# Two cached attentions at one decode step: from 217 tile loads to one stream in 62 KiB rows

## The chip, the cores and the metric

The kernel runs on one core of a Trainium2 chip. The metric is the device time of one execution in microseconds; three timed runs of the kernel before gave 1029.24, 1029.28 and 1032.6 us (median 1029.28 us). The engines are named as the profile names them: PE is TensorE (PEld its weight loads), DVE is VectorE, ACT is ScalarE, POOL is GpSimd, SP is SyncE, which here only issues DMAs. All data is float32.

## The reference, cut to what matters

Two attention blocks read one query token `x` (448 values). Block A has 16 heads with 16 key and value caches; block B has 16 query heads over 8 caches, so that two heads share one. A sigmoid gate mixes both outputs.

```
g = sigmoid((x * gate_w).sum())
for each block:                       # A: 16 caches, B: 8 caches, two heads each
    q = x @ wq                        # 448 -> 16 heads of 256
    scores = q . k_cache * 256**-0.5  # 8192 keys a head
    p = softmax(scores)
    o = p @ v_cache                   # 8192 values a head
    out = concat(o) @ wo              # 4096 -> 448
return g * out_A + (1 - g) * out_B
```

Each cache of one head is 8192 x 256 floats, 8 MiB, and there are 24 key caches and 24 value caches. With the weights that makes 432 MB, each byte of which is read once and used in one or two multiplications.

## The kernel before, in words

The work goes in 8 steps (`NS`). A step `s` holds one cache of B with its two heads (called unit 2) and two heads of A (units 0 and 1), in this order: 2, 0, 1. A cache is cut into 4 tiles (`NT`) of 2048 keys or values: 128 partitions of 4096 floats, 16 KiB a partition and 2 MiB a tile. So the loop `for i in range(N + 1)` (L343) has 96 rounds; in each, SP issues the load of key tile i and of value tile i-1, and now and then the projection weights `wq` (with 14 KiB a partition for a step) and the output weights `wo`. All these loads go into one ring of 11 slots of 16 KiB a partition (`slot`, L74). SP takes the loads in the order in which the program names them and waits ahead of each until its slot is free and an earlier load has landed; at most eight are under way.

A key tile is scored on PE (`scores`, L170). The keys lie turned in memory, so that a matmul with the 32-wide query weights `qb` gives 512 scores to each of four row groups. After each tile DVE takes the minimum (L183) and caps it (L185), ACT exponentiates (L187), and DVE turns the result (L190) into weights for the value matmuls (`attend`, L194, L203). Every tile has a minimum of its own; `combine` and `column` (L232, L265) weight the tiles' sums against each other once a unit has all four. `take` copies the sums out of PSUM, `project_o` makes a column of 256 out of them, and `emit` (L291) multiplies this with `wo` into `Y`. Blocks A and B go the same way.

At the end of the program the last value tile of A is loaded in three pieces (`LAST_CUT`) and the last `wo` in seven: three quarters of it as one load, the last quarter in loads of 96, 12, 8, 6, 4 and 2 partitions (`LAST_ROWS`, L368), 3584 bytes a partition each.

Of the kernel before, what the change touches and what calls it, by code (L numbers as in the profile page):

```python
# [14 lines left out]
P = 128  # L15
# [3 lines left out]
NCOL = SK // P  # L19
# [7 lines left out]
NT = NCOL // ROWS  # L27
BLK = 32
NB = ROWS
R = 4  # L30
OFF = -1.0e5
SLOTS = 11
WQ = (2 * KF + 1) * DH
UNITS = [2, 0, 1]
LAST_CUT = [8, 4, 4]
HEAD_AT = {2: 0, 0: 2, 1: 3}
LAST_ROWS = [96, 12, 8, 6, 4, 2]
# [3 lines left out]
def kernel(  # L41
    ctx: ExitStack,
    tc: tile.TileContext,
    x: bass.AP,
    gate_w: bass.AP,
    a_k: bass.AP,
    a_v: bass.AP,
    b_k: bass.AP,
    b_v: bass.AP,
    wq: bass.AP,  # L50
    wo: bass.AP,
# [8 lines left out]
    ps_sc = ctx.enter_context(tc.tile_pool(name="ps_sc", bufs=2, space=PSUM))  # L60
    ps_o = ctx.enter_context(tc.tile_pool(name="ps_o", bufs=3, space=PSUM))
# [4 lines left out]

    def heads(u):
        return 2 if u[1] == 2 else 1

    def of(u, a, b):  # L70
        s, r = u
        return b[s] if r == 2 else a[2 * s + r]

    def slot(shape, name):  # L74
        t = ring.tile([P, ROWS * DH], F32, name="slot")
        n = 1
        for d in shape:
# [21 lines left out]
    row_of = const.tile([P, R], F32, name="row_of")
    nc.vector.tensor_reduce(row_of, pos.rearrange("p g r -> p r g"), axis=AX.X, op=OP.add)  # L100
    MASK, CAP = {}, {}
    for M in (2, 1):
        MASK[M] = const.tile([P, R // M], F32, name=f"mask{M}")
        nc.vector.tensor_reduce(MASK[M], row_of.rearrange("p (t m) -> p t m", m=M), axis=AX.X, op=OP.add)

        CAP[M] = const.tile([P, R // M], F32, name=f"cap{M}")
        nc.vector.tensor_scalar(CAP[M], MASK[M], 3.0e38, OFF, op0=OP.mult, op1=OP.add)
# [30 lines left out]
    Y = ps_y.tile([P, YN], F32, name="Y")

    def prepare():  # L140
        clear(Y, YN)
        gp = ps_s.tile([1, 1], F32, name="sm")
        for c in range(KF + 1):
            nc.tensor.matmul(gp, xs[:, c:c + 1], gw[:, c:c + 1], start=(c == 0), stop=(c == KF))
        ge = const.tile([1, 1], F32, name="ge")
        nc.scalar.activation(ge, gp, AF.Exp, scale=-1.0)
        nc.vector.tensor_scalar(ge, ge, 1.0, None, op0=OP.add)
        nc.vector.reciprocal(gate[:, 0:1], ge)
        nc.vector.tensor_scalar(gate[:, 1:2], gate[:, 0:1], -1.0, 1.0, op0=OP.mult, op1=OP.add)

    KT, VT, ST, PR, O, GS, SEL, OB, OC = ({} for _ in range(9))

    def project(u, w):

        s, r = u
        M = heads(u)
        q = ps_s.tile([P, 2, 2], F32, name="sm")
        n = 2 * DH
        for m in range(M):
            h = m if r == 2 else r  # L160
            for e in range(2):
                for c in range(KF):
                    at = c * n + h * DH + e * P
                    nc.tensor.matmul(q[:, e, m:m + 1], w[:, at:at + P], xs[:, c:c + 1], start=(c == 0), stop=False)  # L164
                at = KF * n + e * P
                nc.tensor.matmul(q[:, e, m:m + 1], w[:, at:at + P], xs[:, KF + h:KF + h + 1], start=False, stop=True)  # L166
        qb = QB[s % 2, r]
        nc.vector.tensor_scalar(qb[:, :, 16:16 + M], q[:, :, :M], -scale, None, op0=OP.mult)  # L168

    def scores(u, t, kt):  # L170
        M = heads(u)
        if t == 0:
            ST[u] = small.tile([P, 2, NT], F32, name="st", bufs=3)
        sc = ps_sc.tile([P, NB * BLK], F32, name="sc")
        qb = QB[u[0] % 2, u[1]]
        for e in range(2):
            for g in range(NG):
                at = 16 - R * g - t * M % R
                nc.tensor.matmul(sc[32 * g:32 * (g + 1), :], qb[:, e, at:at + 32], kt[:, e, g, :],  # L179
                                 start=(e == 0), stop=(e == 1), skip_group_check=True)  # L180
        st = ST[u]
        mn = small.tile([P, 1], F32, name="mn")
        nc.vector.tensor_reduce(mn, sc, axis=AX.X, op=OP.min)  # L183
        tt = t % (R // M)
        nc.vector.tensor_tensor(st[:, 0, t:t + 1], mn, CAP[M][:, tt:tt + 1], op=OP.min)  # L185
        px = small.tile([P, NB * BLK], F32, name="px")
        nc.scalar.activation(px, sc, AF.Exp, bias=st[:, 0, t:t + 1], scale=-1.0, accum_out=st[:, 1, t:t + 1])  # L187
        pr = small.tile([P, NB * BLK], F32, name="pr")

        nc.vector.transpose(pr.rearrange("p (q r k) -> p q k r", r=BLK, k=2),  # L190
                            px.rearrange("p (q k c) -> p q k c", c=BLK, k=2))
        PR[u, t] = pr.rearrange("p (q c) -> p q c", c=2 * BLK)

    def attend(u, t, j0, n, vt):  # L194
        M = heads(u)
        part, tt = divmod(t, R // M)
        if tt == 0 and j0 == 0:
            O[u, part] = ps_o.tile([P, 2 * DH], F32, name="o")
            clear(O[u, part], 2 * DH)
        pr = PR[u, t]  # L200
        for j in range(j0, j0 + n, 2):
            g = j // 2 % NG
            nc.tensor.matmul(O[u, part][32 * g:32 * (g + 1), :], pr[:, j // 2, :2 * NG * R], vt[:, j - j0:j - j0 + 2, :],  # L203
                             start=False, stop=(tt == R // M - 1 and j >= NB - 2 * NG), skip_group_check=True)

    def take(u, t, last=False):

        M = heads(u)
        part, tt = divmod(t, R // M)
        if tt != R // M - 1:  # L210
            return
        o = O.pop((u, part))
        ob1 = small.tile([P, DH], F32, name="ob1")
        ob = small.tile([P, DH], F32, name="ob", bufs=4)
        if last:
            nc.scalar.activation(ob1, o[:, DH:], AF.Copy)  # L216
            nc.vector.tensor_copy(ob, o[:, :DH])  # L217
            OB[u] = [(ob, SELH[0]), (ob1, SELH[1])]
        else:
            nc.scalar.activation(ob1, o[:, DH:], AF.Copy, scale=half[:, 1:2])  # L220
            nc.vector.scalar_tensor_tensor(ob, o[:, :DH], half[:, 0:1], ob1, op0=OP.mult, op1=OP.add)  # L221
            OB.setdefault(u, []).append((ob, None))
# [254 lines left out]
```

## Time and profile before

| | before |
|---|---|
| median of three runs | 1029.28 us |
| profiled execution, first to last instruction | 1027.5 us |
| what lies around it (median less span) | 1.8 us |
| bytes read from HBM | 432.0 MB |
| rate over the span; in its middle | 420 GB/s; 427 GB/s |
| PE, DVE, ACT busy | 65%, 21%, 10% |
| mean granted TensorE clock | 0.767 |

For the profiled execution the record holds its span and no separate time. How to read it: a DMA of 128 rows is spread over 16 DMA engines, and a "packet" is what one engine moves as one piece: a row of a load, or a 4-byte semaphore update. "Share of 16 engines" is the time that packets took against 16 times the stretch; packets of one engine can overlap a little, so that a share may be over 100%. "GB/s" is what was moved. In groups of instructions, a fp32 matmul is two PE instructions, so `x16` is 8 matmuls of the program.

### The profile page before, as it was taken

The numbers are of one execution on the slowest core, as the hardware profiler recorded it, in microseconds if no ns is written. First come the engines' busy times: TensorE is split into PE (matmuls) and PEld (weight loads), VectorE is DVE, ScalarE is ACT, GpSimd is POOL, SyncE is SP. The second block draws the span as 40 slices with busy tenths as digits, with TensorE's granted clock in tenths as the row PEclk, the third lists the DMA queues.
The fourth block names the chain that finished last, engine by engine and source line by source line (L and its number), as shares of the span: only waits on it lengthen the run. The fifth ranks groups of instructions, "written<-read, shape, count | busy, mean of one in ns | idle before, by whom it ended". The sixth has DMA issues, their size and how long they took to land.

```text
span 1027.5 us, 10697 instructions
## 1 busy us (share of the span) xinstructions
PE 665.1 (65%) x4493; PEld 247.8 (24%) x4493; DVE 215.3 (21%) x650; ACT 98.7 (10%) x258; POOL 0.6 (0%) x6
## 2 busy tenths in 40 slices
PE   5669665696556855567556685556856568555656
PEld 3316111251112411133111251113311123111112
DVE  2121212222212212122121121221212112122222
ACT  1010001000010001000010010100101001010000
POOL 0000000000000000000000000000000000000000
PEclk9777776767766887678786688878787878887877
DMA  9999999999999999999999999999999999999996
GB/s 381 428 427 427 427 425 429 427 426 428 424 429 425 427 425 428 428 428 425 425 428 425 427 427 426 426 428 427 427 429 426 426 426 427 425 427 428 425 428 251
DMA packets 30903, 432.71 MB, mean 421 GB/s; under 512 B 3720, under 2 KB 3720, under 8 KB 4360
## 3 DMA queue, kind: packets, MB, share of 16 engines
q1 hardware_dynamic: 30568, 432.03, 99.3%
q8 instruction: 36, 0.59, 0.2%
q14 instruction: 11, 0.09, 0.0%
q10 hardware_dynamic: 288, 0.00, 0.0%
HBM read 432.02 MB, written 0.00 MB: 420 GB/s over the span
## 4 chain that ended last, share of the span: by engine, by line
DMA 97%; PE 2%; issue 0%; DVE 0%; SPq 0%; ACT 0%
DMA slot<-in_a_v_dram 57%; DMA slot<-in_a_k_dram 15%; DMA slot<-in_b_v_dram 13%; DMA slot<-in_b_k_dram 11%; PE o L203 1%; PE sc L179 0%; PE sm L164 0%; PE sm L286 0%; PE Y L296 0%; PE sm L166 0%; SPq L320 0%; DVE ob L217 0%; SPq L308 0%; ACT ob L216 0%; PE sm L270 0%
## 5 line engine op out<-in xcount | busy, mean ns | idle before, releaser
L203 PE MATMUL o<-slot,pr 128*32 128x512 f32 x1536 | 264.1, 816 | 205.0 <-DMA slot<-in_a_v_dram 139.7
L179 PE MATMUL sc<-slot,qb 128*32 128x512 f32 x1536 | 260.1, 807 | 145.9 <-DMA slot<-in_b_k_dram 84.4
L203 PEld LDWEIGHTS o<-slot,pr 128*32 128x32 f32 x1536 | 57.2, 132 | 377.5 <-issue 193.2
L183 DVE TENSOR_REDUCE mn<-sc 128x1 f32<-128x512 f32 x96 | 66.4, 691 | 376.2 <-PE sc L179 376.1
L187 ACT ACTIVATE px<-sc,st 128x512 f32<-128x512 f32 x96 | 66.0, 688 | 773.7 <-DVE st L185 773.7
L179 PEld LDWEIGHTS sc<-slot,qb 128*32 128x32 f32 x1536 | 54.6, 129 | 253.9 <-issue 239.3
L190 DVE STREAM_TRANSPOSE pr<-px 128x512 f32<-128x512 f32 x96 | 68.4, 713 | 89.0 <-ACT px L187 89.0
L164 PEld LDWEIGHTS sm<-xs,slot 128*128 128x128 f32 x384 | 61.7, 239 | 32.1 <-issue 25.3
L164 PE MATMUL sm<-xs,slot 128*128 128x1 f32 x384 | 65.5, 286 | 5.7 <-DMA slot<-in_wq_dram 5.7
L221 DVE SCALAR_TENSOR_TENSOR ob<-o,half,ob 128x256 f32<-128x256 f32 x31 | 14.9, 480 | 97.2 <-ACT ob L220 97.2
L166 PE MATMUL sm<-xs,slot 128*128 128x1 f32 x128 | 27.6, 285 | 0.0
L286 PEld LDWEIGHTS sm<-sel,ob 128*128 128x128 f32 x124 | 21.3, 248 | 20.5 <-issue 20.5
L278 DVE COPY sel<-sm 128x1 f32<-128x1 f32 (+1 forms) x23 | 3.7, 160 | 102.1 <-PE sm L270 102.1
L166 PEld LDWEIGHTS sm<-xs,slot 128*128 128x128 f32 x128 | 24.8, 240 | 0.0
L220 ACT ACTIVATE ob<-o,half 128x256 f32<-128x256 f32 x31 | 14.7, 474 | 103.9 <-PE o L203 72.6
L270 PEld LDWEIGHTS sm<-one,wr 1*128 1x128 f32 x96 | 16.4, 241 | 30.9 <-issue 29.2
L286 PE MATMUL sm<-sel,ob 128*128 128x2 f32 (+1 forms) x124 | 22.9, 298 | 0.0
L168 DVE TENSOR_SCALAR qb<-sm 128x2 f32<-128x2 f32 (+1 forms) x24 | 3.9, 162 | 79.7 <-PE sm L166 79.7
L270 PE MATMUL sm<-one,wr 1*128 1x1 f32 x96 | 18.5, 292 | 1.8 <-DVE wr L258 1.8
L187 ACT ACTIVATION_READ_ACCUMULATOR px<-sc,st 128x1 f32 x96 | 18.5, 193 | 0.0
L185 DVE TENSOR_TENSOR st<-mn,cap 128x1 f32<-128x1 f32 x96 | 15.3, 160 | 3.3
L136 PE MATMUL o<-zero 128*128 128x512 bf16 x32 | 15.7, 490 | 0.0
(48 smaller groups left out, 104.6 us busy)
## 6 DMA issues: line engine op xcount, KB each, us to landing
slot<-in_a_k_dram SPq DMA_DIRECT2D x64, 2048.0 KB, 38.9
slot<-in_a_v_dram SPq DMA_DIRECT2D x63, 2048.0 KB, 39.2
slot<-in_b_k_dram SPq DMA_DIRECT2D x32, 2048.0 KB, 39.1
slot<-in_b_v_dram SPq DMA_DIRECT2D x32, 2048.0 KB, 38.6
slot<-in_wq_dram SPq DMA_DIRECT2D x7, 1792.0 KB, 38.0
slot<-in_wo_dram SPq DMA_DIRECT2D x7, 1792.0 KB, 39.2
slot<-in_wq_dram SPq DMA_DIRECT2D x2, 896.0 KB
slot<-in_wo_dram SPq DMA_DIRECT2D x1, 1344.0 KB, 29.4
```

What stands on the lines that cost most here:

```text
L136: nc.tensor.matmul(t[:, :n], zero[:, :P], zero[:, :n], start=True, stop=False, skip_group_check=True)
L164: nc.tensor.matmul(q[:, e, m:m + 1], w[:, at:at + P], xs[:, c:c + 1], start=(c == 0), stop=False)
L166: nc.tensor.matmul(q[:, e, m:m + 1], w[:, at:at + P], xs[:, KF + h:KF + h + 1], start=False, stop=True)
L179: nc.tensor.matmul(sc[32 * g:32 * (g + 1), :], qb[:, e, at:at + 32], kt[:, e, g, :], start=(e == 0), stop=(e == 1), skip_group_check=True)
L183: nc.vector.tensor_reduce(mn, sc, axis=AX.X, op=OP.min)
L185: nc.vector.tensor_tensor(st[:, 0, t:t + 1], mn, CAP[M][:, tt:tt + 1], op=OP.min)
L187: nc.scalar.activation(px, sc, AF.Exp, bias=st[:, 0, t:t + 1], scale=-1.0, accum_out=st[:, 1, t:t + 1])
L190: nc.vector.transpose(pr.rearrange("p (q r k) -> p q k r", r=BLK, k=2), px.rearrange("p (q k c) -> p q k c", c=BLK, k=2))
L203: nc.tensor.matmul(O[u, part][32 * g:32 * (g + 1), :], pr[:, j // 2, :2 * NG * R], vt[:, j - j0:j - j0 + 2, :], start=False, stop=(tt == R ...
L221: nc.vector.scalar_tensor_tensor(ob, o[:, :DH], half[:, 0:1], ob1, op0=OP.mult, op1=OP.add)
L270: nc.tensor.matmul(cl[:, a, m:m + 1], WR[M][:, m, a].rearrange("p c x k -> p (c x k)"), one, start=True, stop=True)
L286: nc.tensor.matmul(oc[:, e, :M], ob[:, e::2], sel, start=(k == 0), stop=(k == len(terms) - 1))
```

## The change

The program is written anew around one input. The host lays every cache tile and weight block in the order of use into one flat array, `stream`; each load takes the next 15872 floats a partition (63488 bytes, `FILL`), whatever lies in them. There are 52 such loads, and then two slots that are filled in four pieces each (`TAIL`): 22528, 16384, 16384 and 7680 bytes a partition, and 5376, 3584, 1344 and 448. Every piece has 128 rows. The ring has 3 slots of 62 KiB a partition. The load into a slot is issued when the last item in the slot's earlier content has been used. `pieces` finds for an item (a tile, a weight block) the one, two or more parts of slots in which it lies.

The order of the items is written out in `order()`: in the steps after the first, A's key tiles come one in three or four items, between value tiles of A and tiles of B, and in the first step one in two or three.

Scores of A are made by DVE: the keys lie as rows, `tensor_tensor` multiplies a tile in place with the query (spread over all partitions by PE, in PSUM), and `tensor_reduce` sums 256 products to a score. All four tiles of a head stand in one 128x64 tile `s`. B's scores stay on PE, but all four tiles write one PSUM bank (rows 2t and 2t+1 of each group). So minimum, exponential and turning come once a head pair and no longer once a tile, with one minimum for all keys of a head; `combine`, `column` and the masks are gone, and the sum is divided out by `rz` in `narrow`. The queries are now made with `x` as the weights and `wq` as the moving operand, 512 columns a matmul. The last `wo` is used block by block as its pieces land.

The diff, cut to its core:

```diff
-SLOTS = 11
-UNITS = [2, 0, 1]
-LAST_CUT = [8, 4, 4]
-LAST_ROWS = [96, 12, 8, 6, 4, 2]
+FILL = 31 * UNIT
+SLOTS = 3
+TAIL = [[11 * UNIT, 8 * UNIT, 8 * UNIT, 2 * UNIT + 896], [1344, 896, 336, 112]]
...
+def order():
+    out = [("wq", 0, 0, 0)]
...
+        if s == 0:
+            out += k(0, 0) + k(2, 0, 1) + k(0, 1) + k(2, 2) + k(0, 2) + k(2, 3) + k(0, 3)
+            out += v(2, 0, 1) + k(1, 0) + v(2, 2, 3) + k(1, 1) + v(0, 0, 1) + k(1, 2) + v(0, 2)
+            out += k(1, 3) + v(0, 3) + [("wq", 1, 0, 0)]
+            continue
+        out += k(0, 0) + v(1, 0, 1, of=s - 1) + k(0, 1) + v(1, 2, 3, of=s - 1)
+        out += k(0, 2) + k(2, 0, 1) + k(0, 3) + k(2, 2, 3) + [("wo", s - 1, 0, 0)]
+        out += k(1, 0) + v(0, 0, 1) + k(1, 1) + v(0, 2, 3)
+        if s < NS - 1:
+            out += [("wq", s + 1, 0, 0)] + k(1, 2) + v(2, 0, 1) + k(1, 3) + v(2, 2, 3)
+        else:
+            out += k(1, 2) + v(2, 0) + k(1, 3) + v(2, 1, 2, 3) + v(1, 0, 1, 2, 3) + [("wo", s, 0, 0)]
+    return out
...
+    def load(n):
+        t = ring.tile([P, FILL], F32, name="slot")
+        o = 0
+        for size in FILLS[n]:
+            a = (starts[n] + o) * P
+            nc.sync.dma_start(t[:, o:o + size], stream[a:a + size * P].rearrange("(p f) -> p f", p=P))
+            o += size
+        slots[n] = t
...
+    def scores_a(s, r, t, a):
+        if t == 0:
+            S[s, r] = small.tile([P, NT * ROWS], F32, name="s", bufs=3)
+        q = QA[s][:, r * DH:(r + 1) * DH]
+        for d, n, v in pieces(a, TILE):
+            j, n = d // DH, n // DH
+            v = v.rearrange("p (j d) -> p j d", d=DH)
+            nc.vector.tensor_tensor(v, v, q[:, None, :].to_broadcast([P, n, DH]), op=OP.mult)
+            nc.vector.tensor_reduce(S[s, r][:, t * ROWS + j:t * ROWS + j + n], v, axis=AX.X, op=OP.add)
...
+    def scores_b(s, t, a):
...
+                mm(sc[BLK * g:BLK * (g + 1), :], qb[s % 2][:, e, R - 2 * t:R - 2 * t + BLK], v[:, o:o + UNIT],
+                   start=(t == 0 and e == 0), stop=(t == NT - 1 and e == 1))
...
+    def take(s, r, both=False):
+        o = O[OF.pop((s, r))]
+        ob = small.tile([P, UNIT], F32, name="ob")
+        n = DH if both else UNIT
+        nc.scalar.activation(ob[:, :n], o[:, :n], AF.Copy)
+        if both:
+            nc.vector.tensor_copy(ob[:, n:], o[:, n:])
...
+        if i == last:
+            emit_last(s, a)
+            todo = list(blocks(s, a))
+            for b, l in todo[:6]:
+                emit_block(b, l)
+            narrow(s, 1)
+            for b, l in todo[6:]:
+                emit_block(b, l)
+        while gone < len(ends) and a + SIZE[kind] >= ends[gone]:
+            gone += 1
+            if nxt < len(FILLS):
+                load(nxt)
+                nxt += 1
```

Three places where instructions move. First the end of SP's queue, before (at the end of a row stand partitions by floats, so `128x4096` is one tile):

```order
L320 DMA slot<-in_a_k_dram 128x4096
L329 DMA slot<-in_a_v_dram 128x4096
L362 DMA slot<-in_a_v_dram 128x2048
L362 DMA slot<-in_a_v_dram 128x1024 x2
L336 DMA slot<-in_wo_dram 128x2688
L368 DMA slot<-in_wo_dram 96x896
L368 DMA slot<-in_wo_dram 12x896
L368 DMA slot<-in_wo_dram 8x896
L368 DMA slot<-in_wo_dram 6x896
L368 DMA slot<-in_wo_dram 4x896
L368 DMA slot<-in_wo_dram 2x896
```

and the same place in the changed kernel:

```order
L112 DMA slot<-in_stream_dram 128x15872 [waits DMAHW1_49,DVE_49,PE_49]
L112 DMA slot<-in_stream_dram 128x5632 [waits DMAHW2_49,DVE_49,PE_49]
L112 DMA slot<-in_stream_dram 128x4096 x2
L112 DMA slot<-in_stream_dram 128x1920
L112 DMA slot<-in_stream_dram 128x1344 [waits DMAHW3_49,DVE_49,PE_49]
L112 DMA slot<-in_stream_dram 128x896
L112 DMA slot<-in_stream_dram 128x336
L112 DMA slot<-in_stream_dram 128x112 [waits DMAHW4_49]
```

Loads of a few partitions are gone, and a refill now waits for DVE and PE, the last readers of its slot.

Second, DVE in the middle of a step. Before, over two key tiles (`mn` minimum, `pr` turned weights, `qb` query weights, `gs` sums of a unit):

```order
L183 TENSOR_REDUCE mn<-sc 128x1
L185 TENSOR_TENSOR st<-mn,cap_95 128x1
L190 STREAM_TRANSPOSE pr<-px 128x8x2x32
L227 TENSOR_TENSOR gt_469<-st,mask_93 128x8
L230 TENSOR_REDUCE gs<-gt_469 128x2
L168 TENSOR_SCALAR qb_114<-sm 128x2
L183 TENSOR_REDUCE mn<-sc 128x1
```

and in the changed kernel, over two key tiles of A and the softmax that follows the second:

```order
L234 TENSOR_TENSOR slot<-slot,q 128x4096
L235 TENSOR_REDUCE s<-slot 128x16
L330 TENSOR_TENSOR ocs<-sm,rz 128x2
L234 TENSOR_TENSOR slot<-slot,q 128x1024
L235 TENSOR_REDUCE s<-slot 128x4
L234 TENSOR_TENSOR slot<-slot,q 128x3072
L235 TENSOR_REDUCE s<-slot 128x12
L238 TENSOR_REDUCE low<-s 128x1
L253 TENSOR_REDUCE low<-sc 128x1
```

A tile of A is now two DVE instructions over 4096 floats a partition (or four, where the tile lies in two slots), and no work of PE.

Third, PE at the end of the changed kernel, from the last two matmuls of the last value tile on (`DMAHW` waits are for landings of the stream's pieces):

```order
L96 MATMUL o_122<-slot,p 2x512 [waits DMAHW0_49]
L96 MATMUL o_122<-slot,p 2x512
L96 MATMUL Y<-ysum,ones 1x112 [waits DVE_49]
L96 MATMUL Y<-ysum,ones 1x112 x3
L96 MATMUL Y<-slot,ocs 1x112 x8
L96 MATMUL Y<-slot,ocs 1x112 [waits DMAHW1_49]
L96 MATMUL Y<-slot,ocs 1x112 [waits DMAHW2_49]
L96 MATMUL sm<-pick_a,ob 128x1 [waits Activation_49]
L96 MATMUL Y<-slot,ocs 1x112 [waits DVE_49]
L96 MATMUL Y<-slot,ocs 1x112 [waits DMAHW3_49]
L96 MATMUL Y<-slot,ocs 1x112 [waits DMAHW4_49]
```

Between these rows stand further matmuls of the same form. Six of the eight blocks of `wo` now stand ahead of the last head's `narrow` (`sm<-pick_a,ob`), where before all of `Y` came after it.

More of the change, by code (lines that the diff above doesn't have):

```diff
@@ L99 @@
[L99 to L107, printed above, removed]
@@ L138 @@
[L138 to L149, printed above, removed]
@@ L151 @@
[L151 to L160, printed above, removed]
-            for e in range(2):
[L162 to L176, printed above, removed]
-            for g in range(NG):
[L178 to L222, printed above, removed]
@@ new lines @@
+    nc.vector.memset(ones, 1.0)
+    par = const.tile([P, 2, P], F32, name="par")
+    nc.vector.tensor_copy(par, half[:, :, None].to_broadcast([P, 2, P]))
+    alt = const.tile([1, 2, P], F32, name="alt")
+    nc.vector.memset(alt, 0.0)
+    for m in range(2):
+        nc.vector.memset(alt[:, m].rearrange("p (g r) -> p g r", g=NG)[:, :, m:R:2], 1.0)
+    qb = [const.tile([P, 2, R + BLK], F32, name=f"qb{k}") for k in range(2)]
+    for t in qb:
+        nc.vector.memset(t, 0.0)
+    x = xs[:, :KF + 1]
@@ new lines, with queries @@
+    nc.vector.tensor_scalar(pick_b, row_of[:, :4].rearrange("p (m k) -> p k m", k=2), gs[:, 1:2], None, op0=OP.mult)
+    QA, SC, S, PR, RZ, OB, OC, OF = ({} for _ in range(8))
+    def queries(s, a):
+        qa = ps_q.tile([P, UNIT], F32, name="q")
+        row = ps_sc.tile([P, UNIT], F32, name="sc")
+        for pair, (o, w) in enumerate(((qa, P), (row[:1, :], 1))):
+            blocks = [(c * UNIT, UNIT, c, 0) for c in range(KF)]
+            blocks += [(KF * UNIT, DH, KF + h, h * DH) for h in range(2)]
+            first = True
+            for b, n, c, col in blocks:
+                for d, m, v in pieces(a + pair * WQ + b, n):
+                    mm(o[:, col + d:col + d + m], xr[:, c, :w], v, start=first, stop=(c == KF + 1 and d + m == n))
+                    first = False
+        QA[s] = qa
+        qrow = small.tile([1, UNIT], F32, name="qrow", bufs=1)
+        nc.scalar.activation(qrow, row[:1, :], AF.Copy)
+        return qrow
@@ new lines, in turn @@
+    def turn(s, qrow):
+        qt = ps_s.tile([P, 2, 2], F32, name="sm")
+        for e in range(2):
+            for m in range(2):
+                mm(qt[:, e, m:m + 1], qrow[:, m * DH + e * P:m * DH + (e + 1) * P], ones[:1, :1], start=True, stop=True)
+        nc.vector.tensor_copy(qb[s % 2][:, :, R:R + 2], qt)
+    def scores_a(s, r, t, a):
[7 more added lines that the diff above has]
+            nc.vector.tensor_reduce(S[s, r][:, t * ROWS + j:t * ROWS + j + n], v, axis=AX.X, op=OP.add)
+        if t == NT - 1:
+            low = small.tile([P, 1], F32, name="low")
+            nc.vector.tensor_reduce(low, S[s, r], axis=AX.X, op=OP.min)
+            OF[s, r] = low
@@ new lines, in blocks, with emit, emit_last @@
+    def blocks(s, a):
+        for h, (r, m) in enumerate(((2, 0), (2, 1), (0, 0), (1, 0))):
+            for e in range(2):
+                yield a + (2 * h + e) * D, lambda r=r, m=m, e=e: OC[s, r][:, e, m:m + 1]
+    def emit(s, a):
+        for b, l in blocks(s, a):
+            for d, n, v in pieces(b, D):
+                mm(Y[:1, d:d + n], l(), v, stop=(s == NS - 2))
+    def emit_last(s, a):
+        ysum = small.tile([1, D], F32, name="ysum", bufs=1)
+        nc.vector.tensor_copy(ysum, Y[:1, :])
+        for g in range(NG):
+            mm(Y[BLK * g:BLK * g + 1, :YN], ones[:1, :1], ysum[:, g * YN:(g + 1) * YN], start=True)
@@ L338, with emit_block, after @@
+    def emit_block(b, l):
+        for d, n, v in pieces(b, D):
+            for g in range(NG):
+                lo, hi = max(d, g * YN), min(d + n, (g + 1) * YN)
+                if lo < hi:
+                    mm(Y[BLK * g:BLK * g + 1, lo - g * YN:hi - g * YN], l(), v[:, lo - d:hi - d])
+    items, a = [], 0
+    for it in order():
+        items.append((it, a))
+        a += SIZE[it[0]]
+    assert a == TOTAL
+    ends = [s + sum(f) for s, f in zip(starts, FILLS)]
     later = {}
-    def at(step, f, *args):
+    def after(step, f, *args):
@@ new lines @@
+    nxt = SLOTS
+    gone = 0
+    last = len(items) - 1
+    for i, ((kind, s, r, t), a) in enumerate(items):
+        if kind == "wq":
+            qrow = queries(s, a)
+            after(i, turn, s, qrow)
+        elif kind == "k":
+            if r == 2:
+                scores_b(s, t, a)
+            else:
+                scores_a(s, r, t, a)
+            if t == NT - 1:
+                after(i + (1 if r == 2 else 2), softmax, s, r)
+        elif kind == "v":
+            attend(s, r, t, a)
+            if t == NT - 1:
+                end = i == last - 1
+                take(s, r, both=end)
+                if not end:
+                    after(i + 1, narrow, s, r)
+        elif s < NS - 1:
+            emit(s, a)
```

439 lines of the change are left out of this document (196 added, 243 removed).

## The prediction, made before the change was run

> **What bounds the kernel now.** I read the page first, then the chain of waits, the DMA view in two stretches, a table of stretches over the end, and the timeline there. On the page:
>
> ```profile
> span 1027.5 us, 10697 instructions
> PE 665.1 (65%) x4493; PEld 247.8 (24%) x4493; DVE 215.3 (21%) x650; ACT 98.7 (10%) x258; POOL 0.6 (0%) x6
> ...
> GB/s 381 428 427 427 427 425 429 427 426 428 424 429 425 427 425 428 428 428 425 425 428 425 427 427 426 426 428 427 427 429 426 426 426 427 425 427 428 425 428 251
> ...
> q1 hardware_dynamic: 30568, 432.03, 99.3%
> q8 instruction: 36, 0.59, 0.2%
> ...
> DMA 97%; PE 2%; issue 0%; DVE 0%; SPq 0%; ACT 0%
> ```
>
> No compute engine is busy over 65%; the chain that ended last is DMA for 97%, and 38 of 40 slices move 424 to 429 GB/s. So 432.03 MB at 427 GB/s, 1011.8 us, is the kernel; the rest is start and end. An edit counts only if it moves bytes faster, shortens the two ends, or stops the stream. SP's waits say who holds a load back:
>
> ```profile
> SPq L329 <- DMA slot<-in_a_v_dram: 201.2, 45, 4.7
> ...
> SPq L320 <- PE sc L179: 1.5, 4, 0.7
> ```
>
> It waits for earlier landings; for PE nearly never. The stream is limited inside DMA.
>
> **The rate, step by step.** Bytes stay the same; what changes is the number of packets. The DMA view in the middle (300 to 900 us), and then in the last stretch (1021.55 to 1022.70 us), in which only 3584-byte rows of the last `wo` are left; last the rows of the start (3.0 to 4.6 us), with 7168-byte rows:
>
> ```profile
> DMA packets 17741, 256.02 MB, mean 427 GB/s; under 512 B 1968, under 2 KB 1968, under 8 KB 1968
> q1 hardware_dynamic: 17713, 255.61, 100.4%
> ...
> DMA packets 29, 0.08 MB, mean 65 GB/s; under 512 B 8, under 2 KB 8, under 8 KB 29
> q1 hardware_dynamic: 29, 0.08, 16.6%
> ...
> q1 hardware_dynamic: 88, 0.63, 94.2%
> q10 hardware_dynamic: 51, 0.00, 1.8%
> ```
>
> Tiny packets: 1.8% of 16 x 1.6 us over 51 is 9 ns each. Middle: 100.4% of 16 x 600 us is 9638 us; without 1968 tiny ones 15,745 packets of 16,234 bytes take 0.6110 us each. End: 16.6% of 16 x 1.15 us is 3.05 us; without 8 tiny ones 21 packets of 3584 bytes take 0.142 us each. The line through both has 0.0371 us per 1000 bytes and a fixed 9 ns a packet; from the start's row (0.274 us for 7168 bytes) to the middle it is 7.6 ns. I take 9, from the row in which the engines are least pressed.
>
> The 211 loads of 128 rows and 128 single rows before are 27,136 large packets; the change has 60 pieces of 128 rows, 7,680. The 19,456 that go save 9.1 ns each on one of 16 engines: 11.1 us. Some 2,450 semaphore updates (16 a load) go as well, at 9 ns: 1.4 us. Together **12.5 us**, which makes 432 GB/s. From below the gain could be zero: rows of 63 KB lie four times beyond any row here. From above, 9 ns may be low by some ns, 15 us.
>
> The Trainium skill ("DMA: Bandwidth & Descriptors", "Why small descriptors are slow") gives a fixed cost of about 3 cycles a packet, and calls packetizing worth it only up to 256 bytes. With the 850 MHz of "Where 436 GB/s comes from" that is an estimate of 3.5 ns, 4.3 us instead of 11.1: it speaks against the change, and is in the rivals. The trace's 9 ns is more than twice that, by the rows above.
>
> **The end of the stream.** Stretches:
>
> ```profile
> 1012.00:1014.00 2.00, 1.53 (x16) 0.58 (x17) 0.92 (x3) 0.78 (x2) 0.00 (x0) 1.00 1.02 267
> 1014.00:1016.00 2.00, 0.43 (x8) 0.13 (x3) 1.05 (x6) 0.27 (x1) 0.00 (x0) 1.00 0.69 243
> 1016.00:1018.00 2.00, 1.80 (x12) 0.64 (x14) 0.40 (x3) 0.00 (x0) 0.00 (x0) 0.84 0.63 237
> 1018.00:1020.00 2.00, 2.00 (x8) 0.19 (x4) 0.00 (x0) 0.00 (x0) 0.00 (x0) 0.50 0.57 226
> 1020.00:1022.00 2.00, 1.06 (x5) 0.34 (x3) 0.42 (x1) 0.38 (x1) 0.00 (x0) 0.80 0.28 104
> 1022.00:1028.00 6.00, 2.41 (x71) 2.12 (x70) 0.43 (x2) 0.00 (x0) 0.00 (x0) 0.97 0.03 10
> ```
>
> From 1012 us on 2.2 MB come in 10.7 us; at 427 GB/s they need 5.2. The 5.5 us have two causes: loads of 2 to 12 rows, which use few engines (they go), and engines that run out of step, so that some finish early (the 60% share before the small loads are alone). The second stays in part; fewer PE instructions mean fewer than the 36 instruction packets. I take half, **2.8 us**; bounds 0 and 5.5. The last byte moves from about 1022.7 to 1022.7 - 12.5 - 2.8 = 1007.4 us.
>
> **What follows the last byte.** The timeline of the end:
>
> ```profile
> 1016.48 4.24 PE L203 MATMUL o<-slot,pr 128*32 128x512 f32 x16
> ...
> 1020.76 0.38 ACT L216 ACTIVATE ob<-o 128x256 f32<-128x256 f32 x1 [5.82 <-PE o L203]
> 1021.18 0.42 DVE L217 COPY ob<-o 128x256 f32<-128x256 f32 x1 [4.25 <-ACT ob L216]
> ...
> 1021.66 1.10 PE L286 MATMUL sm<-selh,ob 128*128 128x1 f32 x8 [0.94 <-DVE ob L217]
> ...
> 1022.69 1.71 PE L296 MATMUL Y<-slot,ocs 128*1 128x112 f32 x64
> 1022.80 0.16 DVE L288 COPY ocs<-sm 128x2 f32<-128x2 f32 x1 [1.20 <-PE sm L286]
> 1024.47 0.28 DVE L417 COPY ys<-Y 128x112 f32<-128x112 f32 x1 [1.51 <-PE Y L296]
> ```
>
> Now 4.8 us pass from the last byte to 1027.5. In the changed kernel the last part of a value tile comes 2688 floats a partition earlier (1.376 MB, 3.2 us at 432). After it: two matmuls, two rounds of 0.68 (below), 1.3, `take` on ACT 0.38 and DVE 0.42, the copy of `Y` (448 floats, by DVE's rate below) 0.63, its spreading 8 of 64 such PE instructions 0.21, six blocks of `wo` (48 of 64) 1.28, `narrow` 1.10 and 0.16, two blocks 0.43, `ys` 0.28, the output as now 2.75 (1024.75 to 1027.5), handoffs of 0.05 to 0.1 us some 0.6: 9.5 us. So 6.3 us after the last byte, **1.5 more** than now. Six blocks ahead of `narrow` are what makes it longer.
>
> **What could stop the stream.** Groups of the page:
>
> ```profile
> L179 PE MATMUL sc<-slot,qb 128*32 128x512 f32 x1536 | 260.1, 807 | 145.9 <-DMA slot<-in_b_k_dram 84.4
> L183 DVE TENSOR_REDUCE mn<-sc 128x1 f32<-128x512 f32 x96 | 66.4, 691 | 376.2 <-PE sc L179 376.1
> L221 DVE SCALAR_TENSOR_TENSOR ob<-o,half,ob 128x256 f32<-128x256 f32 x31 | 14.9, 480 | 97.2 <-ACT ob L220 97.2
> L185 DVE TENSOR_TENSOR st<-mn,cap 128x1 f32<-128x1 f32 x96 | 15.3, 160 | 3.3
> ```
>
> DVE: 160 ns for one element and 691 for 512 make 1.04 ns an element, so a sum over 4096 takes 4.4 us. For two inputs L221 gives (480 - 160)/255, 1.25 ns: 5.3 us. The product of a tile is between 4.4 and 5.3, a tile 8.8 to 9.7 us, 64 tiles 570 to 620 us: DVE goes from 21% to about 60%. PE loses 64 of 96 score tiles at 260.1/96 = 2.7 us, 173 us; it gains the wide queries (8 matmuls of 512 columns or 16 instructions, at 2.7/4 = 0.68 us a round 11 us a step) and `emit` in one row group. Both cost nothing while a slot is free before its queue runs dry.
>
> A load of 8.13 MB takes 18.8 us; slot n must be free when load n+2 has landed, 37.6 us after its own. Mean need: 8 tiles of A a step of 24 tiles, 78 us of DVE in 119. The first step is densest. Slot 0 lands at about 2.9 + 18.8 = 21.7 (the first slice's 381 GB/s leave out 2.8 us of its 25.7). PE makes queries 11 us, after the constants; among the start's 88 large packets came 51 of the other queue, so I let their input's rows alternate with those of 63 KB, and PE start at 26: 37. DVE: tile 1 to 47, the two of slot 1 to 66, slot 2's first to 76, two softmaxes some 3, and three quarters of the next to 87. Slot 0 is due at 59 (free 48), slot 1 at 78 (66), slot 2 at 97 (87 to 90). The tightest is 7 to 10 us early, so I cost it at 0; without this cover each us late adds a us. SP's own issue is hidden by two queued loads.
>
> **Sum.** 1027.5 - 12.5 - 2.8 + 1.5 = 1013.7 us of span; the runs' median lies 1.8 above the span, hence **1015.5 us**, 1.3% less.
>
> **Rivals.**
> 1. Large rows bring less than the line says. With nothing for packets (only tiny ones 1.4) the sum is 1026.6: no change. With a third of the 9 ns, 3.7 us instead of 11.1, it is 1022.9. For both: the extrapolation by four. Against: three sizes lie near one line. 10% and 8%. (The Trainium skill's 3 cycles come near the second.)
> 2. Engines stay in step, as a ring of three loads lets none run far ahead, and the whole 5.5 us go, with packets at the upper bound: 1010. For it: the end's stretches; against: instruction packets still fall on single engines. 14%.
> 3. Slower: DVE's product takes two clocks an element (it reads PSUM and writes over its input at once, which no row shows). A tile is then 8.7 + 4.4 = 13.1 us; slot 2 gets free at 37 + 5 tiles less a quarter = 99 + 3, 5 us late, and the lag goes on through the first step, about 20 us; at the end the last keys are late by 10. That makes some 1045. It decides from about 11.5 us a tile on. Against: L221 with two inputs, one of them in PSUM, shows 1.25 ns. 6%.
> 4. PE at half clock at the end: granted 0.50 at 1018 to 1020 us. Seven value tiles in the last 19 us then need 4.2 us each (the 16 instructions at 1016.48) instead of 2.7, 29 us, and PE ends some 8 us late: 1023. For it: PE waits more than before. Against: it works without a pause there, and the same table has it at 1.00 from 1012 to 1016 us. 8%.
>
> The forecast itself has 54%.
>
> **Numbers.** A measurement of this kernel tells 0.5%, 5 us, from no change: faster is below 1024.1. Forecast, rival 2, rival 1's third and most of rival 4 are there (54 + 14 + 8 + 6), less a little for mixtures: 0.80. Rival 1's zero and the rest of 4 give 0.13 for no change; rival 3 and unknown stalls 0.07. The range of 1007 to 1028 holds the forecast, rivals 1, 2 and 4, and leaves out rival 3 and what is beyond.
>
> **What would show it.** Right: 431 to 433 GB/s in the middle, some 8,700 packets, no slice below 9 before the last, DVE near 60% with 4096-wide products of 4.4 to 5.3 us, SP waiting for landings or early releases, last byte at 1005 to 1010 and 6 us behind it. Wrong: 427 GB/s (rival 1); slices below 9 with SP waiting for DVE (3); value matmuls that run on behind the last landing (4).

## The result and the profile after

| | before | after |
|---|---|---|
| median, beside each other on one chip | 1029.26 us (4 runs) | 1013.36 us (4 runs, 1013.18 to 1013.38) |
| ratio to before | | 0.984 [0.9826, 0.9854] |
| profiled execution: its time; its span | span 1027.5 us | 1013.38 us; 1011.6 us |
| last byte of the stream, about | 1022.7 us | 1005.1 us |
| from there to the end of the span | 4.8 us | 6.5 us |

The forecast was 1015.5 us; the time came 2.1 us below it, inside the range. The page of the changed kernel:

```profile
span 1011.6 us, 6308 instructions
PE 535.4 (53%) x2839; PEld 156.0 (15%) x2839; DVE 597.7 (59%) x298; ACT 37.6 (4%) x106; POOL 0.7 (0%) x6
...
GB/s 402 440 442 425 422 437 439 437 427 427 434 435 440 429 427 429 437 432 432 432 437 432 428 437 430 435 432 427 437 440 427 425 434 437 437 429 432 427 424 262
...
q1 hardware_dynamic: 8648, 432.02, 98.9%
q8 instruction: 22, 0.36, 0.1%
...
DMA 62%; DVE 24%; PE 11%; another core or an unknown queue 1%; ACT 1%; issue 0%; SPq 0%
```

The bytes are the same, 432.02 MB, in 8648 packets instead of 30,568, and no slice before the last falls below 402 GB/s. DVE is busy 59% instead of 21%, PE 53% instead of 65%. The chain's shares look as if DVE now carried a quarter of the time, and SP's waits say the same at first sight (engine, line, what it waited for, then us in all, times, longest):

```profile
SPq L112 <- DVE s L235: 943.7, 51, 41.8
```

This is no loss. SP waits for DVE to free a slot while earlier loads, each 18.8 us long, are still being moved. By the packet records (the trace's start, length and size of every packet) the first engine to run out of work still had 5.8 us of it at the tightest refill and 16.8 at the median one. The DMA view over 300 to 900 us shows that the queue does not run dry:

```profile
DMA packets 4612, 259.52 MB, mean 433 GB/s; under 512 B 512, under 2 KB 512, under 8 KB 512
...
q1 hardware_dynamic: 4596, 259.29, 100.0%
```

So it is 433 GB/s in place of 427, with 100.0% of the 16 engines' time in packets. Without the 512 small ones (4.6 us at the prediction's 9 ns) 4084 packets of 63,488 bytes share 9595 us: 2.35 us each. DVE's two instructions for a tile of A, from the groups by shape:

```profile
L235 DVE TENSOR_REDUCE s<-slot 128x16 f32<-128x4096 f32 x48 | 212.2, 4420 | 1.7
L234 DVE TENSOR_TENSOR slot<-slot,q 128x4096 f32<-128x4096 f32 x48 | 211.8, 4412 | 67.5 <-DMA slot<-in_stream_dram 67.5
```

A tile takes 8.83 us. The product with one input in PSUM, written over its other input, is as fast as the sum that reads one input: the low end of the range given for it. The end, in stretches (length, busy time with instructions of PE, PEld, DVE, ACT and POOL, granted PE clock, DMA share, GB/s), and in the timeline:

```profile
1000.00:1002.00 2.00, 1.77 (x16) 0.21 (x8) 0.00 (x0) 0.00 (x0) 0.00 (x0) 1.00 0.64 252
1002.00:1004.00 2.00, 1.03 (x4) 0.09 (x4) 0.32 (x1) 0.38 (x1) 0.00 (x0) 1.00 0.47 181
1004.00:1006.00 2.00, 1.32 (x52) 1.13 (x56) 0.62 (x2) 0.00 (x0) 0.00 (x0) 1.00 0.14 48
```

```profile
1002.19 1.03 PE L96 MATMUL o<-slot,p 128*2 128x512 f32 x4 [0.42 <-DMA slot<-in_stream_dram]
1003.26 0.38 ACT L316 ACTIVATE ob<-o 128x256 f32<-128x256 f32 x1 [10.17 <-PE o L96]
1003.68 0.42 DVE L318 COPY ob<-o 128x256 f32<-128x256 f32 x1 [8.35 <-ACT ob L316]
1004.02 0.60 DVE L347 COPY ysum<-Y 1x448 f32<-1x448 f32 x1
1004.97 1.33 PE L96 MATMUL Y<-slot,ocs 128*1 128x112 f32 x48
1006.24 1.16 PE L96 MATMUL sm<-pick_a,ob 128*128 128x1 f32 x8
1007.64 0.93 PE L96 MATMUL Y<-slot,ocs 128*1 128x112 f32 x16 [0.25 <-DVE ocs L330]
1008.97 0.65 SPq L412 DMA_DIRECT2D out_dram<-ys  x1
```

From 1000 us on 0.96 MB come (the three rates by 2 us). At 433 GB/s that is 2.2 us, and it takes 5.1: 2.9 us are still lost where 5.5 were before. Behind the last value piece everything runs in one line, from PE through ACT, DVE and PE to the output, as the prediction listed it. Of the 15.9 us by which the span is shorter, 17.6 are in the stream, and 1.7 are given back behind it.

### The profile page after: what moved, and what is told of

The parts are those of the page before. It is cut to its first block, busy times and chain, and to the rows that moved or that the text cites. A ratio compares the mean times of both kernels' runs of the same rounds, so it can differ in the third digit from the quotient of the medians.

```text
span 1011.6 us, 6308 instructions
## 1 busy us (share of the span) xinstructions
PE 535.4 (53%) x2839; PEld 156.0 (15%) x2839; DVE 597.7 (59%) x298; ACT 37.6 (4%) x106; POOL 0.7 (0%) x6
## 3 DMA queue, kind: packets, MB, share of 16 engines
q1 hardware_dynamic: 8648, 432.02, 98.9%
HBM read 432.02 MB, written 0.00 MB: 427 GB/s over the span
## 4 chain that ended last, share of the span: by engine, by line
DMA 62%; DVE 24%; PE 11%; another core or an unknown queue 1%; ACT 1%; issue 0%; SPq 0%
DMA slot<-in_stream_dram 62%; DVE s L235 12%; DVE slot L234 12%; PE sc L96 3%; PE o L96 3%; PE sm L96 2%; PE q L96 2%; PE Y L96 2%; ACT px L277 0%; ACT p L286 0%; SPq L112 0%; DVE least L264 0%; ACT bias L272 0%; DVE low L253 0%
## 5 line engine op out<-in xcount | busy, mean ns | idle before, releaser
L234 DVE TENSOR_TENSOR slot<-slot,q 128x4096 f32<-128x4096 f32 (+5 forms) x80 | 284.7, 3559 | 102.0 <-DMA slot<-in_stream_dram 102.0
L235 DVE TENSOR_REDUCE s<-slot 128x16 f32<-128x4096 f32 (+5 forms) x80 | 285.3, 3567 | 2.8
L96 PE MATMUL o<-slot,p 128*2 128x512 f32 x1024 | 177.3, 797 | 189.8 <-DMA slot<-in_stream_dram 189.8
L96 PE MATMUL sc<-slot,qb 128*32 128x512 f32 x512 | 90.2, 820 | 105.7 <-DMA slot<-in_stream_dram 105.4
L96 PE MATMUL o<-slot,pr 128*4 128x512 f32 x512 | 83.8, 777 | 78.3 <-DMA slot<-in_stream_dram 78.3
L96 PEld LDWEIGHTS o<-slot,p 128*2 128x2 f32 x1024 | 28.8, 99 | 317.9 <-DMA slot<-in_stream_dram 211.2
L96 PE MATMUL Y<-slot,ocs 128*1 128x448 f32 (+3 forms) x178 | 54.6, 501 | 12.3 <-DMA slot<-in_stream_dram 12.0
L96 PEld LDWEIGHTS sc<-slot,qb 128*32 128x32 f32 x512 | 19.9, 142 | 166.9 <-DMA slot<-in_stream_dram 114.1
L96 PE MATMUL q<-slot,xr 128*128 128x512 f32 (+1 forms) x80 | 35.5, 598 | 0.0
L96 PE MATMUL sc<-slot,xr 128*1 128x512 f32 (+1 forms) x80 | 28.8, 507 | 0.0
L96 PE MATMUL sm<-ident,low 128*1 128x128 f32 x48 | 10.8, 312 | 17.6 <-DVE low L238 16.8
```

The lines of the kernel that those rows point to most:

```text
L96: nc.tensor.matmul(o, l, r, start=start, stop=stop, skip_group_check=True)
L234: nc.vector.tensor_tensor(v, v, q[:, None, :].to_broadcast([P, n, DH]), op=OP.mult)
L235: nc.vector.tensor_reduce(S[s, r][:, t * ROWS + j:t * ROWS + j + n], v, axis=AX.X, op=OP.add)
```

## The experiments

The theory was the prediction's: a fixed cost for every packet, engines out of step and few-row loads at the end, a serial tail, and compute that is hidden as long as slots come free in time. Each run takes one term apart. All are edits of the changed kernel; the ratio is always to the kernel before on the same chip.

### The price of a packet: rows in 4 and in 16 packets

Each full row of 63,488 bytes is laid as 4 (or 16) pieces that stand apart in HBM. A load remains one DMA of the same bytes into the same slot; only its packets become 15,872 (3968) bytes.

```diff
+CUT = 4        # 16 in the second run
...
-nc.sync.dma_start(t[:, o:o + size], stream[a:a + size * P].rearrange("(p f) -> p f", p=P))
+c = CUT if size == FILL else 1
+nc.sync.dma_start(t[:, o:o + size].rearrange("p (c f) -> p c f", c=c),
+                  stream[a:a + size * P].rearrange("(c p f) -> p c f", c=c, p=P))
...
```

> The changed kernel, but each 62 KiB row of the 52 full loads is moved as 4 packets of 15872 bytes, by one DMA as before; compute is untouched. Theory (a fixed 9 ns a packet): 8 x 3 x 52 = 1248 more packets on each engine, 11.4 us more: 1024.7 us, 427 to 428 GB/s in the middle. Rival 1 with a third of the fixed cost: 4 us more, 1017. Rival (the gain comes from one contiguous stream and fewer DMAs, not from row length): 1013.4, 433 GB/s.

> As cut4 with 16 packets of 3968 bytes a row, still one DMA a load. Theory (9 ns a packet): 8 x 15 x 52 = 6240 more packets on each engine, 57 us more: 1070 us, about 408 GB/s. With a third of that cost: 1032. Rival (stream and number of DMAs): 1013.4.

| packets | median | ratio | over the changed kernel | more packets on each engine | ns each |
|---|---|---|---|---|---|
| 63,488 B (the changed kernel) | 1013.36 us | 0.984 [0.9826, 0.9854] | | | |
| 15,872 B | 1026.26 us | 0.9959 [0.9945, 0.9973] | 12.9 us | 52 x 8 x 3 = 1248 | 10.3 |
| 3968 B | 1072.06 us | 1.0399 [1.038, 1.0417] | 58.7 us | 52 x 8 x 15 = 6240 | 9.4 |

(By the ratios, which take out the difference of the chips, the first difference is 0.0119 x 1030, 12.3 us, 9.8 ns.) The DMA view over 300 to 900 us, of 15,872-byte packets and then of 3968-byte ones:

```profile
DMA packets 16660, 256.29 MB, mean 427 GB/s; under 512 B 512, under 2 KB 512, under 8 KB 512
```

```profile
DMA packets 62221, 245.11 MB, mean 409 GB/s; under 512 B 494, under 2 KB 494, under 8 KB 62205
...
q1 hardware_dynamic: 62205, 244.87, 102.3%
```

The engines are full each time, and the rate falls from 433 to 427 and 409 GB/s. With 15,872-byte packets it is the rate of the kernel before, whose packets were of 16 KB. So the gain in the middle is the packets' fixed cost, 9 to 10 ns, over a factor of 16 in size. This settles rival 1: the line does not bend up to 62 KB. The packet records say so directly: in this stretch packets of 63,488, 15,872 and 3968 bytes last 2350, 597 and 159 ns, which lie on one line of 36.8 ns per 1000 bytes and 13 ns a packet; as packets of one engine overlap a little (the shares over 100%), 9 to 10 of the 13 ns are paid. A packet is in all these runs also one unbroken piece of HBM, so that a cost of each packet and a cost of each such piece are not told apart. Of the whole gain about 4 us remain with four times the packets (1026.26 against 1030.19 us); they belong to the end of the stream and to whatever else the change removed.

### The number of loads

The same 15,872-byte rows, but as four DMAs, each of 128 rows, instead of one.

```diff
+m = size // c          # c = 4 for a full slot
+for k in range(c):
+    nc.sync.dma_start(t[:, o + k * m:o + (k + 1) * m],
+                      stream[a + k * m * P:a + (k + 1) * m * P].rearrange("(p f) -> p f", p=P))
...
```

> As cut4 in packets (15872 bytes), but each slot is filled by 4 DMAs instead of one: 156 more DMAs and 2496 more semaphore updates. Theory (packets): cut4's time plus 156 x 9 ns = 1.4 us on each engine, 1026. Rival (the number of DMAs is what cost): clearly above cut4, and cut4 near 1013.

1026.98 us, 0.9968 [0.9958, 0.9978]; 0.7 us above the single DMA by the medians, 0.9 us below it by the profiled spans (1024.9 and 1025.8). The DMA view over 300 to 900 us:

```profile
DMA packets 18151, 256.13 MB, mean 427 GB/s; under 512 B 2013, under 2 KB 2013, under 8 KB 2013
```

Against the cut rows in one DMA there are 1501 more small packets in this stretch, semaphore updates, and the rate is again 427. For the 156 more DMAs of the whole kernel, 2496 updates, the prediction's price is 1.4 us. The two intervals overlap, so that the times neither show nor refute this 1.4 us. The packet records put the last byte at 1018.8 us here and at 1017.7 with one DMA, 1.1 us later, which is near it; the spans come out the other way because PE's work behind the last byte took 8.1 us in the profiled execution with one DMA, at a granted clock of 0.50 from 1018 us on, and 6.1 here. So by these two executions 156 more DMAs cost some 1 us, where 1248 more packets on each engine cost 12.

### Engines out of step

To add instruction packets and little else, each value matmul of the first seven steps is followed by four tiny matmuls on zeros, whose result nothing reads. The eighth step, and so the end, has the old program.

```diff
+EXTRA = 4
+if s < NS - 1:
+    for _ in range(EXTRA):
+        mm(Y[96:98, :2], zero[:, :2], zero[:, :2], start=True, stop=True)
```

> The changed kernel with four tiny added matmuls (2 columns, into PSUM rows that nobody reads) after each value matmul of the first seven steps: some 5500 more PE instructions, about 22 more instruction packets of 16 KB, 44 in all, no other bytes. Theory (engines get out of step by the instruction packets that fall on some of them): the last byte comes 3 to 5 us later, 1017 to 1018 us, with the same 433 GB/s in the middle of the stream. Rival (out of step for another reason): 1013 to 1014.

1018.0 us, 0.9877 [0.986, 0.9895]: 4.6 us more than the changed kernel by the medians, 3.8 by the ratios. Its page and its stretches at the end (the profiled execution took 1019.3 us):

```profile
q8 instruction: 43, 0.70, 0.3%
```

```profile
1004.00:1006.00 2.00, 1.87 (x16) 0.32 (x16) 0.00 (x0) 0.00 (x0) 0.00 (x0) 1.00 0.49 202
1006.00:1008.00 2.00, 1.05 (x8) 0.09 (x4) 0.05 (x1) 0.38 (x1) 0.00 (x0) 1.00 0.49 187
1008.00:1010.00 2.00, 1.05 (x31) 0.80 (x35) 0.89 (x2) 0.00 (x0) 0.00 (x0) 0.86 0.14 44
```

From 1000 us on the rate is low in both kernels, but where the changed kernel moves 252, 181 and 48 GB/s in three stretches and is done, this one moves 253, 199, 202, 187 and 44 in five: the stream ends 4.2 us later, at 1009.4. Instruction packets rose from 22 to 43. A packet takes about 1.1 us (0.3% of 16 x 1017.5 us over 43); 21 more of them, shared evenly by 16 engines, would cost 1.5 us. So the engines do not share them evenly: some fall behind and finish alone. The packet records say the same. Between the semaphore updates of the first and the last of the 16 engines to finish a load lie, in the changed kernel, 0.56 us early in the program and 5.1 us at the last full load; it grows in steps, the larger ones of about 1.3 us, little more than one instruction packet. With the added packets it is 9.2 us at the last full load, 4.1 more, and that is the delay of the stream. The 2.9 us still lost at the end of the changed kernel are thus those of engines out of step. That a ring of three loads keeps the engines in step, as rival 2 had it, is refuted.

### The few-row loads at the end

The pieces of the last `wo` are changed so that its last quarter comes as before, in loads of 96, 12, 8, 6, 4 and 2 rows of 3584 bytes. What stands ahead of it in that slot comes as one piece of 7168 bytes a partition; all else stays.

```diff
-TAIL = [[11 * UNIT, 8 * UNIT, 8 * UNIT, 2 * UNIT + 896], [1344, 896, 336, 112]]
+TAIL = [[11 * UNIT, 8 * UNIT, 8 * UNIT, 2 * UNIT + 896], [1792, 896]]
+LAST_ROWS = [96, 12, 8, 6, 4, 2]
...
```

The changed kernel ran beside it on the same chip as `again`.

> The changed kernel with the last quarter of the last wo in loads of 96, 12, 8, 6, 4 and 2 rows, as before the change, in place of pieces of 128 rows. Prediction (about half of the 5.5 us that the end of the stream lost is due to loads of few rows): 2.8 us more, 1016. Rival (engines out of step are nearly all of it; the busiest engine gets 11 of these rows instead of 8, 0.4 us): 1013.5 to 1014.

> The changed kernel itself, beside the next ones on one chip: 1013 to 1014 us.

1015.58 us (1014.43 to 1016.3), 0.9856 [0.9837, 0.9875], against 1012.97 of `again`: 2.6 us more, 2.0 in the profiled spans (1013.3 and 1011.3). The timelines, of the few-row kernel and then of `again`:

```profile
1003.42 1.03 PE L97 MATMUL o<-slot,p 128*2 128x512 f32 x4 [1.05 <-DMA slot<-in_stream_dram]
...
1007.47 1.70 PE L97 MATMUL sm<-pick_a,ob 128*128 128x1 f32 x8
```

```profile
1002.02 1.03 PE L96 MATMUL o<-slot,p 128*2 128x512 f32 x4 [0.42 <-DMA slot<-in_stream_dram]
...
1006.07 1.05 PE L96 MATMUL sm<-pick_a,ob 128*128 128x1 f32 x8
```

1.4 us of it come from the landings: already the value piece ahead of these loads is late by that much, and so is the last byte (1006.3 and 1004.9 us by the packet records). Another 0.65 us is PE's own, at a lower granted clock, as the few-row kernel's stretches show:

```profile
1006.00:1008.00 2.00, 2.00 (x60) 1.60 (x54) 0.00 (x0) 0.00 (x0) 0.00 (x0) 0.92 0.01 2
1008.00:1010.00 2.00, 1.75 (x22) 1.48 (x22) 0.16 (x1) 0.00 (x0) 0.00 (x0) 0.50 0.00 0
```

So few-row loads cost this kernel 2 to 2.6 us, 1.4 of them in the stream. Why they delay a piece that was issued before them stays open. By the packet records single packets are slower for a while: those of the value piece (7680 bytes) averaged 352 ns against 296 in `again`, and the 3584-byte ones 197 ns, against 177 for the same rows in the kernel before and 144 in `again`, where they come as one piece of 128 rows. No run here tells apart what slows them, or what lowers PE's clock behind them.

### DVE without its cover

To price rival 3, each sum over the products is done twice (the second time to the same result), which makes a tile 13.2 us.

```diff
-nc.vector.tensor_reduce(S[s, r][:, t * ROWS + j:t * ROWS + j + n], v, axis=AX.X, op=OP.add)
+for _ in range(2):
+    nc.vector.tensor_reduce(S[s, r][:, t * ROWS + j:t * ROWS + j + n], v, axis=AX.X, op=OP.add)
```

> The changed kernel with each sum of the scores of A done twice (the same result), so that a tile of A takes DVE 13.2 us instead of 8.8, as in rival 3. By rival 3's working the third slot is late by some 5 us, the first step's lag goes on, and the end is late by 10: some 1045. If the ring's cover were larger than worked out there: 1013 to 1020.

1066.94 us (2 runs), 1.0354 [1.0331, 1.0377]: 54 us more than the changed kernel, and 22 above the rival's 1045. The page and two stretches:

```profile
GB/s 420 418 422 267 344 419 315 448 382 368 434 419 456 418 424 451 419 437 435 431 430 436 432 384 420 453 419 439 436 425 444 424 432 434 425 436 432 365 400 38
```

```profile
75.00:100.00 25.00, 9.01 (x46) 3.34 (x46) 16.14 (x10) 0.95 (x3) 0.00 (x0) 0.54 0.84 361
100.00:125.00 25.00, 10.26 (x91) 3.18 (x90) 23.63 (x10) 1.21 (x4) 0.00 (x0) 0.80 0.56 232
```

The stream stops where it was said to, at the refill of the third slot, but for 15 us (0.16 and 0.44 of 25 us) where the working had 5. DVE's timeline shows why. First the changed kernel (of each row the start, length, instruction, and in brackets the idle time ahead of it), then this one:

```profile
72.34 0.22 DVE L238 TENSOR_REDUCE low<-s 128x1 f32<-128x64 f32 x1
...
81.00 0.28 DVE L264 TENSOR_REDUCE least<-sm 1x1 f32<-1x128 f32 x1 [5.00 <-PE sm L96]
...
82.94 3.34 DVE L234 TENSOR_TENSOR slot<-slot,q 128x3072 f32<-128x3072 f32 x1
```

```profile
89.78 0.22 DVE L239 TENSOR_REDUCE low<-s 128x1 f32<-128x64 f32 x1
...
99.30 0.28 DVE L265 TENSOR_REDUCE least<-sm 1x1 f32<-1x128 f32 x1 [5.87 <-PE sm L96]
...
101.25 3.34 DVE L234 TENSOR_TENSOR slot<-slot,q 128x3072 f32<-128x3072 f32 x1
104.62 6.74 DVE L236 TENSOR_REDUCE s<-slot 128x12 f32<-128x3072 f32 x2
```

Two softmaxes hold DVE for 10.6 us in the changed kernel (72.34 to 82.94) and for 11.5 here, most of it idle behind PE and ACT, where both the cover and the rival had "some 3". The third slot is free at 111.4 instead of 102. Further dips follow (slices 5, 7, 9, 10, 24 and 38), which a single lag in the first step had left out. The last minimum over A's scores starts at 987.95 us in the changed kernel and at 1042.35 here, 54 us later, as much as the whole kernel. By then the stream is at its end (it stops at about 1043.6, 38.5 us later than in the changed kernel), and 22 us with a softmax, value sums and the last output weights still follow. So the mechanism of rival 3 is right, and dearer than it was priced; the product's real 4.41 us kept it away.

### A shorter tail

Two things are moved: the spreading of `Y` by PE, together with its copy, goes ahead of the last value tile, and only five blocks of `wo` stand ahead of `narrow`.

```diff
+            if i == last - 1:
+                emit_last(s, a)
...
-            emit_last(s, a)
-            for b, l in todo[:6]:
+            for b, l in todo[:5]:
```

> The changed kernel with its end reordered: the copy of Y and its spreading stand ahead of the last value tile, and the last head's narrow comes after five blocks of wo, with three blocks behind it instead of two. Theory (PE's order behind the last value matmul sets the end, not the last byte): the copy (0.60), the spreading (0.37) and what waits for them leave the chain, 2 us less than the changed kernel: 1011.3. Rival (the last landing at 1005.5 us sets the end): the same as the changed kernel, within 0.5 us.

1011.06 us (1010.9 to 1011.27), 0.9812 [0.9797, 0.9827], 1.9 us below `again` beside it; the same kernel on a second chip 1011.34 us, 0.9807 [0.9793, 0.9821]. Its timeline:

```profile
1000.84 0.37 PE L96 MATMUL Y<-ysum,ones 1*1 1x112 f32 x8
...
1004.53 1.05 PE L96 MATMUL sm<-pick_a,ob 128*128 128x1 f32 x8
...
1006.80 0.65 SPq L413 DMA_DIRECT2D out_dram<-ys  x1
```

The output leaves at 1006.80 instead of 1008.68 in `again`, while the last byte lands at 1005.1 as in the changed kernel. The work behind the last byte was in fact serial, and what could be done earlier had cost its full time. This version beats both kernels.

The next step let the last value piece land 0.46 MB earlier, by moving bytes of `wo` behind it, with `narrow` ahead of all blocks:

```diff
-TAIL = [[11 * UNIT, 8 * UNIT, 8 * UNIT, 2 * UNIT + 896], [1344, 896, 336, 112]]
+TAIL = [[11 * UNIT, 8 * UNIT, 8 * UNIT, 2 * UNIT], [2240, 896, 336, 112]]
...
```

> As the reordered end, and the last value tile's last piece no longer carries two blocks of wo with it (they go into the next piece), so that it lands 0.46 MB or 1.1 us earlier; narrow stands ahead of all eight blocks. Theory (the chain from the last value landing through narrow sets the end): 1 us less than the reordered end, 1010.0. Rival (the last byte, which does not move, and what follows it now set the end): 1011.

> The reordered end again, beside the last one on one chip: 1011 us.

1011.21 us, 0.9807 [0.9792, 0.9821], against 1011.34 us of the shorter tail beside it: no difference. Its timeline:

```profile
1001.34 1.90 PE L96 MATMUL o<-slot,p 128*2 128x512 f32 x16
1003.30 0.38 ACT L316 ACTIVATE ob<-o 128x256 f32<-128x256 f32 x1 [9.18 <-PE o L96]
...
1004.96 1.71 PE L96 MATMUL Y<-slot,ocs 128*1 128x112 f32 x64
1005.06 0.16 DVE L330 TENSOR_TENSOR ocs<-sm,rz 128x2 f32<-128x2 f32 x1 [0.92 <-PE sm L96]
...
1007.07 0.65 SPq L411 DMA_DIRECT2D out_dram<-ys  x1
```

And the shorter tail beside it:

```profile
1005.66 0.89 PE L96 MATMUL Y<-slot,ocs 128*1 128x112 f32 x24
1005.77 0.16 DVE L330 TENSOR_TENSOR ocs<-sm,rz 128x2 f32<-128x2 f32 x1 [1.52 <-PE sm L96]
...
1006.95 0.66 SPq L413 DMA_DIRECT2D out_dram<-ys  x1
```

The expected 1 us did not come, for two reasons that the rows show. ACT's copy starts at 1003.30, where it started at 1003.41 in the shorter tail: the earlier place in the stream hardly brought the value sums earlier. PE works through 16 instructions without a pause from 1001.34 on, so that PE, and no longer the landing alone, sets their end; the spreading of `Y` that now stands ahead of them belongs to what it must do first. And the other move cancels itself: `narrow` stands ahead of all blocks, so that its result `ocs` comes 0.71 us earlier (1005.06 instead of 1005.77), but then eight blocks follow instead of three, 1.71 us instead of 0.89. So it is not the last byte that holds this end, as the rival had it, but PE's own work.

## Why the prediction was right

- **What bounds the kernel.** DMA, before and after. The engines are 100.0% in packets in the middle, with DVE at 59% and PE at 53%.
- **The rate.** 9.1 ns a packet and 432 GB/s were forecast; 9.4 to 10.3 ns and 433 came. This is the term that carried the forecast, and the cut rows reproduce it on its own: 12.3 to 12.9 us for 1248 packets on each engine, almost the number that the change removed (19,456 over 16 is 1216). It rested on a choice: 142 ns for a 3584-byte row came from the last 21 of 128 such rows. All 128 averaged 177 ns by the packet records, which in the same working would have given 54 ns a packet; the runs bear the choice out. The 1.4 us for semaphore updates lie below what the times resolve; the packet records have 1.1. The Trainium skill ("DMA: Bandwidth & Descriptors", "Why small descriptors are slow") gives about 3 cycles a packet, and by the prediction's estimate of 3.5 ns from it the four-packet rows would cost 4.4 us (1248 x 3.5 ns). The measured time is nearly three times that, and decides against the estimate.
- **The end of the stream.** 2.8 us were to come back, and 2.6 did (5.5 less 2.9). The two causes were named rightly, and each was found by itself: few-row loads cost 1.4 us in the stream, and engines out of step are what is still lost. That the rest of the 2.6 us comes from fewer instruction packets (22 instead of 36) fits, but no run shows it alone.
- **After the last byte.** 6.3 us forecast, 6.5 measured.
- **The cover.** No stall of the stream, DVE at "about 60%", and the third slot free at 87 to 90 us: its refill was issued at 89.73, shown by SP's timeline of the changed kernel:

```profile
89.73 0.33 SPq L112 DMA_DIRECT2D slot<-in_stream_dram  x1
```

  But this number is right by errors that cancel, which is luck. DVE started earlier and had done its four tiles by 72.3 us instead of 76, and the two softmaxes took 10.6 us instead of 3. The first tile in DVE's timeline:

```profile
35.01 4.41 DVE L234 TENSOR_TENSOR slot<-slot,q 128x4096 f32<-128x4096 f32 x1
39.46 4.42 DVE L235 TENSOR_REDUCE s<-slot 128x16 f32<-128x4096 f32 x1
```

  It begins at 35.0 instead of 37 and is done at 43.9 instead of 47. With the slower product that the prediction left open (9.7 us a tile) the five tiles would have added 4 us and eaten more than half of the cover to 97. Nor is the first step alone the tightest: by the packet records the first engine had 6.3 us of work left at this refill, 6.4 at one near 709 us, and 5.8 at the last full one. And a step is 54.0 MB, 125 us at 432 GB/s, and not the 119 of the working, so that the mean need was a little smaller than stated there.
- **Rivals.** 1 and 2 fell by the runs above. 4 did not occur: the granted clock is 1.00 from 990 to 1006 us, and falls only behind the last value matmul. 3 did not occur either, but its price was too low by 22 us; the steps at fault are the 3 us for two softmaxes, in which DVE's waits for PE and ACT alone take 9, and the single lag in the first step, which left out the later stalls.
- **The 2.1 us too many.** The last byte came 2.3 us before the forecast, and what follows it took 0.2 longer. 1 GB/s more in the middle is 2.3 us over 432 MB, so it is the rate that came out a little better. A fixed cost of 10 ns instead of 9.1, which the four-packet rows show and the sixteen-packet rows (9.4) hardly do, would be 1.1 us of it; for the rest there is no run.

## What to carry to other kernels

Where the DMA engines are full all the time, count packets: every packet that disappears is worth its fixed cost on one of 16 engines, here 9 to 10 ns for rows of 4 to 62 KB, and the number of DMAs hardly matters. Large loads buy this with a coarse ring, so work out when each slot comes free, the waits between engines included; the margin here was 6 us, and a kernel that used it up lost not the difference but several times that. What follows the last byte is serial and paid in full, so that moving 2 us of work ahead of it gives 2 us.

## What had not been expected of the hardware

- Instruction packets cost more through their unevenness than through their bytes: 21 more of them, 0.34 MB in 432, made the stream 4.2 us longer, where 1.5 us would be their even share, and drove the 16 engines 9.2 us apart instead of 5.1.
- Loads of a few rows at the end delay bytes that were issued ahead of them (1.4 us for the value piece, whose packets took 352 ns instead of 296), and not only their own.
- A multiplication in place with a spread PSUM operand is as fast as a sum over one SBUF input (4412 and 4420 ns for 4096 floats a partition).
- The granted PE clock fell from 0.92 to 0.50 between the two last stretches shown of the few-row kernel, and there `narrow` took 1.70 us instead of 1.05: in a serial tail such a step is paid in full.
